# An identity, a split read and earlier input loads in the prologue of a Fourier filter with a token and channel mixer

## The chip, the cores and the metric

The kernel runs on one core of one Trainium2 chip. The metric is the device time of one execution in microseconds (us), taken on the chip. Executions of one and the same kernel scatter here by 3 to 10 us from the fastest to the slowest, that is 0.1 to 0.4%, so what follows is about differences near the edge of what can be measured. All runs told of here were in the fast state.

## The reference, cut to what matters

```python
def _attn_ref(x, filt_r, filt_i):            # x: 8 x 3008 x 256, float32
    X = np.fft.rfft(x, axis=1)
    Y = X * (filt_r + 1j * filt_i)[None]
    return np.fft.irfft(Y, n=x.shape[1], axis=1).astype(np.float32)

def _moe_ref(x, w_tok1, w_tok2, w_ch1, w_ch2):   # the four weights arrive as 64-bit floats
    xt = x.transpose(0, 2, 1)
    h = np.maximum(xt @ w_tok1, 0.0) @ w_tok2
    u = x + h.transpose(0, 2, 1)
    h2 = np.maximum(u @ w_ch1, 0.0) @ w_ch2
    return (u + h2).astype(np.float32)
```

First a filter along the 3008 tokens by way of a Fourier transform, then a mixer: two products along the tokens, and two along the channels.

## The kernel before

The transform is done as matmuls in two stages (3008 = 47 x 64). A batch's data go out to a buffer in device memory between the stages (`z_tmp`) and after the filter (`g_tmp`). The filter of batch 0 runs alone in the prologue. The filters of the later batches (in groups 1-2, 3-4, 5-6 and 7) are interleaved with the mixer of the batches before. In the prologue the 64-bit weights are also converted: each is split into two 32-bit floats, `top` and `rest`, whose sum is the weight. For most tiles TensorE makes this sum. The stationary matrix is `wai_t` for the first token weight, and an identity for the first six tiles of the second.

```python
def halves(st, n, pair):                      # one tile of 64-bit weights
    nc.scalar.activation(out=top, in_=hi_f, func=AF.Copy, scale=2.0 ** -112)          # ScalarE, L235
    yield
    nc.vector.tensor_scalar(...)                                                      # VectorE, L237
    ...                                                                               # three more, to L242

def on_chip(stat, top, rest, n, parts):
    banks.append(banks.pop(0))
    def f(tag=banks[0]):
        ps = bank(tag)
        m = ident[0] if stat is None else stat
        nc.tensor.matmul(ps[:, 0:n], m, top, start=True, stop=False)                  # L276
        nc.tensor.matmul(ps[:, 0:n], m, rest, start=False, stop=True)
        for src, dst in parts:
            nc.scalar.copy(out=dst, in_=src(ps))                                      # L279
    behind.append((ended[0] - 1, f))          # done two conversions later
...
def a_unit(b, c):                             # a "step" on one input block
    ps = bank(free_bank())
    nc.tensor.matmul(ps, wa, xs.pop((b, c))..., start=True, stop=True)                # L409
    nc.scalar.copy(out=t1..., in_=ps)                                                 # L411
    nc.scalar.dma_start(rows_of(z_d, b)[:, ts(c, XC), :], t1)
...
def t4_load(b, c, lo=0, hi=P):                # reads the filter's result, rows lo to hi, for the mixer
    if lo == 0:
        t4[b, c] = t4p.tile([P, TC4, D], FP32, tag="t4", name="t4")
    nc.sync.dma_start(t4[b, c][lo:hi], rows_of(g_d, b)[lo:hi, ts(c, TC4), :])
```

Rows 4k to 4k+3 of `t4` are ready when step k of the filter (`bi_unit(k)`, k = 0 to 31) has been written to `g_tmp`. The main part of the program:

```python
for i, _ in enumerate(dft(GROUPS[0])):        # the filter of batch 0; LAST_STEP = NXC + 2 + K2
    if i == 0:
        for t, src in ((wai_t, wait_d), (wai, wai_d)):
            nc.scalar.dma_start(t, src)
    ...                                        # conversions in between
        if LAST_STEP - 6 <= i < LAST_STEP:
            t4_load(0, i - LAST_STEP + 6, 0, EARLY_ROWS)        # rows 0 to 95, six reads of 384 KB
ident.append(t4p.tile([P, P], FP32, tag="t4", name="ident"))
nc.sync.dma_start(ident[0], ident_d)
second = dft(GROUPS[1])
next(second)                                   # first input blocks of batches 1 and 2
for c in range(A // TC4):
    t4_load(0, c, EARLY_ROWS)                  # rows 96 to 127
sum_up()
for i in range(rounds, A // 2 + TC * N2 // NG):
    convert()
    if i - rounds < XB:
        next(second)                           # a_unit
    if i == A // 2 + BY_PE - 1:
        sum_up()
        acc = token_sums(0)                    # L523, needs all of t4
...
for b, i, place in mix(next_ready):            # items of the mixer, three places in each
    ...
    if not done and (place == 1 or group == 0 and (spread or place == 2 and i % 2)):
        spread = next(todo, "end")             # a step of the next group's filter
        done = spread == "end"
```

DMAs of `nc.sync` are issued by SP, those of `nc.scalar` by ScalarE between its other instructions, and the filter's tables of batch 0 (`filt`) by GpSimd.

## Time and profile before

| | us |
|---|---|
| time, median of 3 runs | 2592.26 (2589.87 to 2595.21) |
| profiled span | 2587.8 |
| end of the filter of batch 0 on TensorE | 119.7 |
| first conversion on VectorE after it | 133.15 |
| token sums of batch 0 start | 139.54 |
| first mixer item starts | 171.28 |
| token sums of batch 1 start | 496.75 |

The rows below the span are times in the profiled run (from its start), and each kernel below is read at the same points. Where a later marker has moved by as much as an earlier one, nothing between them has been won or lost. The lines that carry the argument stand in the prediction.

### The profile page before, as it was taken

The page shows a single profiled execution, that of the slowest core. Times are in us where ns is not written, and L with a number is a line of the kernel's source. Part 1 is how long each engine was busy: PE and PEld are TensorE (multiplying, and loading weights), DVE is VectorE, ACT ScalarE, POOL GpSimd, SP SyncE. Part 2 cuts the span into 40 slices and gives each one's busy share as a digit, 9 for nine tenths or more (in the row PEclk, how much of TensorE's full clock was granted, in tenths as well). Part 3 has the DMA queues.
Part 4 walks back from the last instruction along what each step waited for, and adds up shares of the span by engine and source line. Part 5 has one row for each costly group of instructions (what it writes and reads, how often), then busy time and mean ns, then how long its engine had stood idle before and what let it go on. Part 6 is the DMA issues. An engine that isn't in the chain of part 4 may idle for free.

```text
span 2587.8 us, 31510 instructions
## 1 busy us (share of the span) xinstructions
PE 2506.3 (97%) x10952; PEld 2002.3 (77%) x10952; DVE 1795.6 (69%) x3441; ACT 691.4 (27%) x1347; POOL 524.7 (20%) x966
## 2 busy tenths in 40 slices
PE   5889999999999999999999999999999999999998
PEld 2456666788878777888787777788888888888887
DVE  3787888556675888746666788846678576647676
ACT  2433222123222222222321222212222122212222
POOL 3653111111211112112112111121121121211212
PEclk8999999999999999999999999999999999999999
DMA  8965333312332332202232223211232121100001
GB/s 235 263 190 166 107 106 107 94 48 87 93 90 63 88 86 73 80 17 89 90 96 78 75 84 87 80 31 57 90 85 75 50 64 52 25 9 8 17 12 21
DMA packets 156650, 211.43 MB, mean 82 GB/s; under 512 B 34552, under 2 KB 105314, under 8 KB 156492
## 3 DMA queue, kind: packets, MB, share of 16 engines
q1 hardware_dynamic: 84444, 118.86, 15.8%
q0 software_dynamic: 30656, 39.93, 6.4%
q10 hardware_dynamic: 41392, 50.62, 6.0%
q8 instruction: 87, 1.43, 0.2%
q14 instruction: 71, 0.58, 0.1%
HBM read 134.31 MB, written 74.97 MB: 81 GB/s over the span
## 4 chain that ended last, share of the span: by engine, by line
PE 80%; DVE 12%; DMA 3%; issue 2%; ACT 2%; ACTq 0%; SPq 0%; POOL 0%; DVEq 0%; POOLq 0%
PE ps_po L614 27%; PE ps_pg L580 16%; PE ps_pg L596 12%; PE ps_acc L540 4%; PE ps_acc L523 3%; PE ps_b L523 2%; DVE t L558 2%; PE ps_b L540 2%; PE ps_acc L477 2%; DVE hh L558 2%; PE ps_acc L545 2%; PE ps_b L452 2%; DVE u L558 2%; PE ps_b L409 2%; PE ps_b L477 1%
## 5 line engine op out<-in xcount | busy, mean ns | idle before, releaser
L558 DVE TENSOR_TENSOR hh<-ps_pg,s 128x512 f32<-128x512 f32 (+3 forms) x864 | 482.1, 585 | 622.6 <-ACT s L583 621.8
L659 POOL DMA_DIRECT2D out_dram<-r x757 | 409.8, 550 | 1943.5 <-ACT hh L601 921.0
L601 ACT ACTIVATE hh<-hh 128x512 f32<-128x512 f32 (+1 forms) x576 | 347.7, 621 | 1111.9 <-DVE hh L558 1111.9
L614 PE MATMUL ps_po<-t,wc 128*128 128x256 f32 (+1 forms) x2304 | 535.4, 375 | 5.4 <-DVE t L558 4.7
L614 PEld LDWEIGHTS ps_po<-t,wc 128*128 128x128 f32 x2304 | 434.4, 190 | 132.4 <-issue 54.0
L580 PE MATMUL ps_pg<-v,wc 128*128 128x256 f32 (+1 forms) x1728 | 416.0, 377 | 1.9 <-POOL wc L330 1.7
L614 PE MATMUL ps_po<-hh,wc 128*128 128x256 f32 (+1 forms) x1728 | 412.9, 375 | 0.2 <-ACT hh L601 0.2
L580 PEld LDWEIGHTS ps_pg<-v,wc 128*128 128x128 f32 x1728 | 328.5, 191 | 42.9 <-DVE v L558 3.0
L614 PEld LDWEIGHTS ps_po<-hh,wc 128*128 128x128 f32 x1728 | 328.2, 190 | 38.8 <-ACT s L583 0.8
L596 PE MATMUL ps_pg<-u,wc 128*128 128x256 f32 (+1 forms) x1152 | 293.2, 377 | 2.4 <-DVE hh L558 1.9
L558 DVE TENSOR_TENSOR t<-t,hh 128x256 f32<-128x256 f32 (+1 forms) x576 | 242.4, 421 | 19.8
L596 PEld LDWEIGHTS ps_pg<-u,wc 128*128 128x128 f32 x1152 | 215.9, 190 | 38.8 <-DVE hh L558 12.3
L558 DVE TENSOR_TENSOR s<-ps_pg,hh 128x512 f32<-128x512 f32 (+1 forms) x288 | 196.0, 681 | 30.7 <-PE ps_pg L580 0.9
L558 DVE TENSOR_TENSOR t<-hh 128x512 f32<-128x512 f32 (+1 forms) x288 | 191.9, 666 | 0.6 <-ACT hh L601 0.6
L580 PE MATMUL ps_pg<-u,wc 128*128 128x256 f32 (+1 forms) x576 | 170.4, 378 | 0.0
L596 PE MATMUL ps_pg<-v,wc 128*128 128x256 f32 (+1 forms) x576 | 168.8, 375 | 0.0
L583 ACT COPY s<-ps_pg 128x256 f32<-128x256 f32 (+1 forms) x288 | 105.8, 367 | 154.5 <-PE ps_pg L580 151.3
L596 PEld LDWEIGHTS ps_pg<-v,wc 128*128 128x128 f32 x576 | 108.7, 190 | 13.1
L580 PEld LDWEIGHTS ps_pg<-u,wc 128*128 128x128 f32 x576 | 102.8, 191 | 17.0 <-issue 8.4
L540 PE MATMUL ps_acc<-w,h 128*128 128x512 f32 (+1 forms) x228 | 106.2, 587 | 3.5 <-DVE w L263 2.8
L477 PE MATMUL ps_acc<-p,wb 128*96 128x256 f32 (+1 forms) x256 | 93.5, 466 | 7.5 <-DVE p L469 2.8
L523 PE MATMUL ps_b<-t,w 128*128 128x256 f32 x384 | 83.8, 380 | 1.3 <-ACT t L483 1.3
(92 smaller groups left out, 2251.8 us busy)
## 6 DMA issues: line engine op xcount, KB each, us to landing
z_tmp<-t ACTq DMA_DIRECT2D x96, 256.0 KB
t<-z_tmp SPq DMA_DIRECT2D x128, 192.0 KB
g_tmp<-t ACTq DMA_DIRECT2D x128, 192.0 KB
x<-in_x_dram SPq DMA_DIRECT2D x184, 128.0 KB
out_dram<-r POOLq DMA_DIRECT2D x698, 32.0 KB, 1.8
t<-g_tmp SPq DMA_DIRECT2D x42, 512.0 KB
wb<-wbi_t SPq DMA_DIRECT2D x80, 224.0 KB
filt<-in_filt_r_dram SPq DMA_DIRECT2D x128, 48.0 KB
```

The lines of the kernel that those rows point to most:

```text
L409: nc.tensor.matmul(ps, wa, xs.pop((b, c)).rearrange("p a d -> p (a d)"), start=True, stop=True)
L452: nc.tensor.matmul(ps, wbs[k // WC][0:KR, k % WC, 0:P], t2s[k // KC][:, k % KC], start=True, stop=True)
L477: nc.tensor.matmul(ps[0:KR], wbs[k // WC][:, k % WC, P:], p, start=(i == 0), stop=(i == len(parts) - 1))
L523: nc.tensor.matmul(acc[:, t, :], w1[:, a, ts(t, P)], t4[b, a // TC4][:, a % TC4, :], start=(a == 0 and t == 0), stop=(a == A - 1 and t == ...
L540: nc.tensor.matmul(ps[:, 0:w], h1[:, t, ts(dh, P)], w2[:, t, ds(m * 512, w)], start=(t == 0), stop=False)
L558: nc.vector.tensor_tensor(out=out, in0=in0, in1=in1, op=op)
L580: nc.tensor.matmul(ps[:, 0:hw], wc1[:, jp, n, :], mov, start=True, stop=True)
L583: nc.scalar.copy(out=s[:, 0], in_=g[0][:, 0, 0:hw])
L596: nc.tensor.matmul(ps[:, 0:hw], wc1[:, jp, n, :], mov, start=True, stop=True)
L601: nc.scalar.activation(out=hs, in_=hs, func=AF.Relu)
L614: nc.tensor.matmul(po[i][:, j, 0:hw], wc2[:, jp, n, :], mov, start=(jp == 0 and first == 1), stop=(jp == JP - 1 and last == 1))
L659: q.dma_start(rows[g, e, :, ds(h * A + 4 * m, n)], blocks[ts(g, CW), h, e, 0:n])
```

## The change

It removes the wait for the identity, has the mixer's first input read in three parts so that less is left to read when the filter ends, and issues the first input blocks of the second group before the last of these parts. A new rule for the steps in the mixer takes two input blocks in each of the items 0 to 3 instead of three.

```diff
-LAST_STEP = NXC + 2 + K2
-EARLY_ROWS = 96
+PARTS = (0, 64, 112)
...
+    ident = h1p.tile([P, P], FP32, tag="h1", name="ident")
...
-                where, tag = (h1p, "h1") if first and c % 3 == 2 else (t3p, "t3")
+                where, tag = (p2p, "p2") if first and c % 3 == 2 else (t3p, "t3")
...
+        second = dft(GROUPS[1])
         for i, _ in enumerate(dft(GROUPS[0])):
             if i == 0:
-                for t, src in ((wai_t, wait_d), (wai, wai_d)):
+                for t, src in ((wai_t, wait_d), (wai, wai_d), (ident, ident_d)):
                     nc.scalar.dma_start(t, src)
...
-                if LAST_STEP - 6 <= i < LAST_STEP:
-                    t4_load(0, i - LAST_STEP + 6, 0, EARLY_ROWS)
-        ident.append(t4p.tile([P, P], FP32, tag="t4", name="ident"))
-        nc.sync.dma_start(ident[0], ident_d)
-        second = dft(GROUPS[1])
-        next(second)
+                k = i - NXC - 2
+                if 19 <= k < 25:
+                    t4_load(0, k - 19, 0, PARTS[1])
+                elif k == 25:
+                    next(second)
+                elif k in (30, 31):
+                    for c in range(3):
+                        t4_load(0, 3 * (k - 30) + c, PARTS[1], PARTS[2])
         for c in range(A // TC4):
-            t4_load(0, c, EARLY_ROWS)
+            t4_load(0, c, PARTS[2], P)
...
-            if not done and (place == 1 or group == 0 and (spread or place == 2 and i % 2)):
+            if not done and (place == 1 or group == 0 and (spread and (place == 2 or i > 3) or place == 2 and i % 2)):
```

The cuts hold only what follows from these lines (`on_chip` gets `ident` as its stationary matrix). The change has four parts, called here the identity, the inputs ahead, the early reads, and the new rule.

> **What bounds the kernel now.** I read the page first. Its busy row says that TensorE is the bound over the span (97%), its clock row that only the first two of the 40 slices (65 us each) run below full clock, and its DMA row that the traffic is dense only there. Whatever the change can win lies in the prologue: the filter of the first batch, the conversion of the weights, and the first steps of the mixer.
>
> ```profile
> PE 2506.3 (97%) x10952; PEld 2002.3 (77%) x10952; DVE 1795.6 (69%) x3441; ACT 691.4 (27%) x1347; POOL 524.7 (20%) x966
> ...
> PE   5889999999999999999999999999999999999998
> ...
> PEclk8999999999999999999999999999999999999999
> DMA  8965333312332332202232223211232121100001
> ```
>
> Second, the timeline of TensorE (columns: start, duration, engine, line, operation, out<-in, shape, count; in brackets the idle time ahead of it and what ended it):
>
> ```profile
> 118.98 0.67 PE L477 MATMUL ps_acc<-p,wb 128*96 128x256 f32 x2 [0.15 <-DVE p L467]
> 126.52 1.62 PE L276 MATMUL ps_po<-both,ident 128*128 128x377 f32 x2 [6.86 <-DMA ident<-ident_t]
> ...
> 135.04 0.80 PE L276 MATMUL ps_po<-both,ident 128*128 128x377 f32 x2
> ...
> 139.54 20.88 PE L523 MATMUL ps_b<-t,w 128*128 128x256 f32 x96
> 161.12 1.12 PE L540 MATMUL ps_acc<-w,h 128*128 128x512 f32 x2 [0.69 <-ACT h L529]
> 165.02 1.13 PE L540 MATMUL ps_acc<-w,h 128*128 128x512 f32 x2 [2.78 <-DVE w L263]
> ```
>
> The filter ends at 119.6. The next matmul needs the identity and waits 6.86 us for it. The token sums (L523) then start at 139.54 with no wait of their own, but after them L540 waits for VectorE's converted weight. So the end of this stage is set by VectorE, and its timeline, with ScalarE's and the DMA queue's, says why it is late:
>
> ```profile
> 120.33 0.55 DVE L242 SCALAR_TENSOR_TENSOR both<-st,both 128x377 f32<-128x377 uint32 x1
> 133.15 0.36 DVE L237 TENSOR_SCALAR both<-both 128x377 uint32<-128x377 uint32 x1 [12.26 <-ACT both L235]
> ...
> 164.16 0.80 DVE L263 TENSOR_TENSOR w<-both 128x192 f32<-128x192 f32 x2
> ```
> ```profile
> 123.04 0.31 ACTq L488 DMA_DIRECT2D g_tmp<-t  x1
> 129.43 0.80 ACT L279 COPY w<-ps_po 128x384 f32<-128x384 f32 x1 [9.37 <-PE ps_po L277]
> 131.94 0.82 ACT L279 COPY w<-ps_po 128x384 f32<-128x384 f32 x1 [1.71 <-PE ps_po L277]
> 132.56 0.56 ACT L235 ACTIVATE both<-st 128x377 f32<-128x377 f32 x1
> ```
> ```profile
> 106.48 4.91 SPq L517 DMA_DIRECT2D t<-g_tmp  x6
> 112.06 0.34 SPq L776 DMA_DIRECT2D ident<-ident_t  x1
> 112.69 11.10 SPq L398 DMA_DIRECT2D x<-in_x_dram  x4
> 129.58 2.63 SPq L517 DMA_DIRECT2D t<-g_tmp  x6
> ```
>
> VectorE stands still for 12.26 us, because the next conversion's first step (ScalarE L235) is queued behind copies of the two sums (L279) that need the identity. From 133.15 VectorE works without a gap to 165, one weight tile each 2.62 us. The identity was issued at 112.06 behind six reads of 384 KB and used at 126.5: 14.4 us for 64 KB. In the merged chain it is the longest piece of the prologue.
>
> **What the Trainium skill says.** "DMA: Bandwidth & Descriptors", section "Queues, rings and completion order": within one queue an engine takes descriptors in order; and "Issuing engines are not separate DMA queues" there: all issuers share the same 16 engines. The trace agrees: 64 KB took 14.4 us where the DMA share between 106 and 120 us is 0.99. So where the identity is issued decides, not its size. The same page, "Rules for kernel authors", says not to split a transfer by partitions, as the parts use the same engines; here a split into three is made so that parts can start before their source is complete, and I expect from it an earlier last part, not more bandwidth. "TensorE: Matmul & The Clock Gate", "What's actually happening": an idle window of about 3.4 us halves the clock. The trace agrees: after the 6.86 us wait the two-matmul group takes 1.62 us, later 0.80.
>
> **The change part by part.**
>
> 1. The identity comes with the first tables, on ScalarE's queue. Added early: one issue (0.3 us of the ACT queue) and 64 KB at about 250 GB/s, 0.26 us, in a stretch where TensorE waits for transfers anyway: cost 0 to 0.5 us. Its buffer is the one that the filter's third output tile used; that tile goes to another single buffer, so nothing is lost. Removed: the wait. The filter ends at 119.6; two sums of 1.27 us each at full clock (135.04 to 136.31 for one) end at 122.2. Before, the second of these ended at 131.7 and VectorE restarted at 133.15, 1.45 us later. So VectorE restarts near 122.2 + 1.45 = 123.6, 9.5 us earlier. From there the chain of conversions is rigid (133.15 to 164.96), so L540 moves from 165.0 to about 155.5.
>
> 2. The token sums must not become the new bound. Three more conversions of 1.85 us after 123.6 allow them at about 129.5 + 0.3. Their last rows, 112 to 127, need the filter's last write. Before, ScalarE's issue of it stood at 123.04 although the tile was copied at 120.06; the order of the instructions with their waits shows that it waited for the landing of one of the big reads that shares its semaphore. After the change it shares with an earlier write, so I expect the issue at 120.4, the landing at about 124, the issue of six reads of 64 KB as long as that of the six before (2.63 us, as it goes by their number), and data at 127 to 129. Even if late: 129.8 + 20.9 + 1 = 151.7 against 155.5, so up to 4 us are hidden.
>
> 3. Reads of rows 0 to 63 (6 x 256 KB = 1.5 MB) move from 106-111 us to about 90-105, where the DMA share is 0.88 already: 0.12 x 18 us = 2.2 us free against 1.5 MB at 285 GB/s = 5.3 us. The filter's own loads may be pushed by some us, of which prefetch two pairs ahead hides most. Against it: the stall of VectorE for a filter table (1.88 us, near 114.9) that the burst before caused may go. I book a loss of 1 us, 0 to 3.
>
> 4. Second group's inputs: two blocks in at about 107 instead of 113-124, used at 122-124 now. No own gain.
>
> 5. In the mixer's first four items two input blocks instead of three are taken per item. Before, TensorE waited for inputs 2.96 us (182.4), 0.54 and 4.17 us (206.6), and two stretches of the items had clock 0.85 and 0.87. But VectorE is busy 11.53 of 12.03, 9.55 of 11.09 and 12.37 of 13.09 us in items 0 to 2, so these waits are mostly hidden: items 0 to 3 take 49.1 us and could take about 44.6. The four blocks that are put off cost 0.86 us each in items 4 to 7, where TensorE has no idle time: 3.4 us back. Net gain 1.1 us.
>
> 6. The first group's filter now ends one and two thirds items later. Before, the last inverse matmul ended at 479.3, the tiles of the next batch were read from 484 on, and its token sums started at 496.7. Now only the rest of one item and one whole item lie between the two: 1.7 + 1.5 + 1.1 + 1.1 + 1.5 = 6.9 us of matmuls by the timeline of such an item at 483 to 497. The first tile needs, as before, about 7.1 us from the end of the inverse matmul (copy 0.6, write and its landing 2.2, issue and read of 0.5 MB 4): 0 to 1 us lost, 0.5 booked.
>
> Sum: -9.5 + 0.3 + 1 - 1.1 + 0.5 = -8.8 us. 2592.26 - 8.8 = 2583.5; I say 2583.
>
> **The rivals.**
> A. The wait for the identity is replaced by one for the last rows of the mixer's input, because DMA is the true bound of 60 to 126 us (share 0.92 to 1.05). For it: density. Against it: the last part shrinks from 768 KB to 384 KB, and 4 us of slack. If true, the token sums start near 136 and the gain is 3 to 4 us: 2588.
> B. The earlier reads starve the filter: TensorE's small gaps at 60-115 grow by 3 to 5 us. For it: the share. Against it: total bytes up to 126 us are the same. Result 2586 to 2588.
> C. The input waits at 182 and 206 are worth their full size with the slow clock (about 11 us). For it: the chain of waits goes through these loads. Against it: VectorE's busy time above. Result 2575 to 2578.
> D. The order helps nothing as a late stage takes it all back. Nothing speaks for it: after 260 us TensorE is 93 to 97% busy and the order of work is fixed.
>
> **Range and chances.** Two runs of the kernel before differ by up to 5.3 us, so noise alone is 2 to 3 us. A and B pull up 4 us, C down 6. Range 2577 to 2588. A gain over 2% would be 52 us, more than all waits of the prologue after 119 us together; a loss over 2% would need a stall that I see nowhere. Faster 0.01, same 0.98, slower 0.01.
>
> **What would show it.** Right: no idle time ahead of L274 (the identity's matmul), VectorE's gap of 12.26 us shrunk to about 3, token sums starting at 129 to 132, the first L538 that waits for a converted weight near 155.5. A shows as a wait of L521 for the input tile; B as an end of the filter after 121; C as items 0 to 3 under 42 us. Point 6 shows as a wait of the second batch's token sums. I am wrong if the filter's end moves by more than 2 us or VectorE restarts later than 126.

## The result, and the profile after

| | before | after |
|---|---|---|
| median of 4 runs, us | 2593.66 (2589.87 to 2595.21) | 2592.15 (2589.95 to 2593.20) |
| ratio | | 0.9995, 95% interval 0.9978 to 1.0013 |

A ratio is the mean time of one kernel's fast runs over that of the other's fast runs of the same rounds, so it isn't quite the ratio of the medians. The times are the same, and 2592.15 lies outside the predicted range of 2577 to 2588.

The timeline of TensorE, of the kernel after (start, duration, engine, line, operation, out<-in, shape, count; in brackets the idle time ahead and what ended it). From `on_chip` on, lines are numbered two lower than before.

```profile
109.48 2.02 PE L475 MATMUL ps_acc<-p,wb 128*96 128x256 f32 x4 [2.69 <-ACT t L481]
...
125.53 1.10 PE L475 MATMUL ps_acc<-p,wb 128*96 128x256 f32 x4 [0.46 <-ACT t L481]
126.47 0.80 PE L274 MATMUL ps_po<-both,ident 128*128 128x377 f32 x2
...
139.31 22.64 PE L521 MATMUL ps_b<-t,w 128*128 128x256 f32 x96 [2.37 <-ACT both L235]
162.65 1.98 PE L538 MATMUL ps_acc<-w,h 128*128 128x512 f32 x4 [0.69 <-ACT h L527]
...
498.74 20.99 PE L521 MATMUL ps_b<-t,w 128*128 128x256 f32 x96 [0.81 <-DMA t<-g_tmp]
```

The same view of VectorE:

```profile
130.40 0.36 DVE L237 TENSOR_SCALAR both<-both 128x377 uint32<-128x377 uint32 x1 [2.88 <-ACT both L235]
...
161.38 0.80 DVE L263 TENSOR_TENSOR w<-both 128x192 f32<-128x192 f32 x2
```

The identity's matmul (L274) has no wait any more, and VectorE's gap has shrunk from 12.26 to 2.88 us. That is the gain that was predicted. But the filter now ends at 126.6 instead of 119.7, so VectorE restarts 2.75 us earlier and not 9.5. The token sums start only 0.2 us earlier and run in part at a slow clock (the clock that TensorE was granted was 0.50 of full from 139.8 to 143.2 us; the 96 matmuls take 22.64 us, before 20.88), and L538, which had waited 2.78 us for VectorE before, now waits for nothing but the token sums themselves. The first mixer item starts at 169.77 (before 171.28), and the second batch's token sums at 498.74 (before 496.75). A prologue 1.5 us shorter is followed by a stretch 3.5 us longer.

Why the filter ends later shows in the waits between 80 us and the filter's end (what waited and for what: us in total, times, longest). Before:

```profile
DVE p L466 <- DMA filt<-in_filt_i_dram: 1.9, 1, 1.9
...
PE ps_acc L477 <- ACT t L483: 1.0, 2, 0.6
```

After:

```profile
ACT filt L215 <- DMA filt<-in_filt_r_dram: 10.1, 6, 1.9
...
PE ps_acc L475 <- ACT t L481: 6.2, 6, 2.7
...
DVE p L464 <- DMA filt<-in_filt_i_dram: 3.7, 2, 2.1
```

ScalarE, which copies half of each filter table (L215), waits 10.1 us for tables to land, where before it waited for none in this stretch. Its instructions run in program order, so its copies of the filter's results (L481) come late, and TensorE waits 6.2 us (before 1.0) for them to free the bank. The transfers of these tables say the same (count, KB each, median us from issue to landing). Before, from 80 to 120 us:

```profile
filt<-in_filt_i_dram POOLq DMA_DIRECT2D x7, 48.0 KB, 4.0
...
filt<-in_filt_r_dram POOLq DMA_DIRECT2D x6, 32.0 KB, 3.3
```

After, from 80 to 127 us:

```profile
filt<-in_filt_i_dram POOLq DMA_DIRECT2D x7, 48.0 KB, 6.1
...
filt<-in_filt_r_dram POOLq DMA_DIRECT2D x7, 32.0 KB, 5.2
```

And what the early reads meet there: the stretch from 88 to 106 us in the view of windows (window, its us, then busy us and instructions of TensorE, its weight loads, VectorE, ScalarE and GpSimd, the granted clock, DMA share, GB/s), before and after:

```profile
88.00:106.00 18.00, 16.91 (x63) 10.21 (x61) 16.75 (x38) 8.83 (x19) 16.06 (x29) 1.00 0.88 247
```
```profile
88.00:106.00 18.00, 15.94 (x58) 9.71 (x59) 14.11 (x32) 7.66 (x17) 13.09 (x25) 1.00 1.02 269
```

The DMA share (the packets' times as a share of 16 engines' span, so that it can pass 1) goes from 0.88 to 1.02, and every engine gets less done in the same 18 us: 63 against 58 matmuls, 38 against 32 instructions of VectorE.

A part of the delay comes from a slower TensorE. From the end of its wait of 2.69 us (matmuls again at 109.48) its granted clock was half of full for 6.83 us, in the same view of windows:

```profile
109.05:115.88 6.83, 6.40 (x13) 4.01 (x14) 4.39 (x10) 1.72 (x4) 4.87 (x9) 0.50 1.06 259
```

It was busy for 6.40 us of these; as an estimate from this line, the same matmuls would have taken up to 3.2 us less at full clock. All four kernels with the early reads (they are told of below) have 6.8 us at half clock between 100 us and the filter's end, and the seven with no read as early have none there.

The way to the token sums after the filter is next. The DMA queue of SP and the DMA queue of ScalarE, after:

```profile
122.58 14.07 SPq L515 DMA_DIRECT2D t<-g_tmp  x12
```
```profile
127.07 0.31 ACTq L486 DMA_DIRECT2D g_tmp<-t  x1
```

The filter's last write is issued right when its tile is copied, as predicted. But the reads behind it are issued up to 136.65, and the token sums have to wait for their data: 139.3 instead of the predicted 129.8. The profile puts this wait to ScalarE's L235, which ended last, at 139.27. By the trace's semaphores L521 waited for the first of the six late reads, whose last piece landed at 139.18, and by the program it needs nothing of L235. What SP's queue waited for between 80 and 145 us (columns as for the waits above):

```profile
SPq L515 <- DMA g_tmp<-t: 18.6, 5, 7.3
```

The longest single wait for a write to `g_tmp`, 7.3 us, is the one for the last write, which landed at 133.98, 6.9 us after its issue. The prediction had booked 3.6 us for this.

### The profile page after: what moved, and what is told of

It reads as the page before. It is cut to its first block, busy times and chain, and to the rows that moved or that the text cites. A ratio compares the mean times of both kernels' runs of the same rounds, so it can differ in the third digit from the quotient of the medians.

```text
span 2590.2 us, 31521 instructions
## 1 busy us (share of the span) xinstructions
PE 2510.2 (97%) x10952; PEld 2002.7 (77%) x10952; DVE 1795.7 (69%) x3441; ACT 691.2 (27%) x1347; POOL 527.7 (20%) x966
## 4 chain that ended last, share of the span: by engine, by line
PE 76%; DVE 12%; ACT 2%; issue 2%; DMA 1%; ACTq 0%; DVEq 0%; POOL 0%; SPq 0%; POOLq 0%
PE ps_po L612 27%; PE ps_pg L578 16%; PE ps_pg L594 11%; PE ps_b L538 4%; PE ps_b L521 3%; DVE t L556 3%; DVE hh L556 2%; PE ps_acc L521 2%; PE ps_acc L538 2%; PE ps_b L543 2%; PE ps_acc L407 2%; DVE u L556 2%; PE ps_acc L475 1%; PE ps_b L475 1%; DVE s L556 1%
## 5 line engine op out<-in xcount | busy, mean ns | idle before, releaser
L521 PE MATMUL ps_b<-t,w 128*128 128x256 f32 x480 | 106.3, 384 | 3.2 <-ACT both L235 2.4
L538 PE MATMUL ps_b<-w,h 128*128 128x512 f32 (+1 forms) x232 | 107.7, 587 | 0.0
```

Source lines behind the costliest of these rows:

```text
L521: nc.tensor.matmul(acc[:, t, :], w1[:, a, ts(t, P)], t4[b, a // TC4][:, a % TC4, :], start=(a == 0 and t == 0), stop=(a == A - 1 and t == ...
L538: nc.tensor.matmul(ps[:, 0:w], h1[:, t, ts(dh, P)], w2[:, t, ds(m * 512, w)], start=(t == 0), stop=False)
```

## The experiments

Theory: the early reads put 1.5 MB on the DMA engines while the filter's tables are being fetched, and the longer filter eats what the early identity wins. Rival one: it is the inputs issued ahead, also in the filter's time, that lengthen it. Rival two: the prologue is better, and the new rule in the mixer gives the gain back. Each run below has a ratio to the kernel before, taken on the same chip in the same call with five rounds. Medians of before were 2593.18 (first four runs), 2592.0 (next four) and 2592.6 (last two). All results were correct.

### The identity alone

The kernel before, with only this part:

```diff
+    ident = h1p.tile([P, P], FP32, tag="h1", name="ident")
-                where, tag = (h1p, "h1") if first and c % 3 == 2 else (t3p, "t3")
+                where, tag = (p2p, "p2") if first and c % 3 == 2 else (t3p, "t3")
-                for t, src in ((wai_t, wait_d), (wai, wai_d)):
+                for t, src in ((wai_t, wait_d), (wai, wai_d), (ident, ident_d)):
-        ident.append(t4p.tile([P, P], FP32, tag="t4", name="ident"))
-        nc.sync.dma_start(ident[0], ident_d)
```

> The kernel before with one part of the change: the identity comes with the first tables (and the third output tile moves to the other single buffer). Theory (the early reads of the mixer's input starve the filter of its tables; the identity is a gain by itself): the filter ends at 119.6 us as before (within 1), VectorE restarts its conversions at 123.5 to 126.5 instead of 133.15, the mixer's first step starts at 162 to 166 instead of 171.3, and the time falls by 5 to 9 us, to 2584 to 2588. Rival 1 (the early identity itself, by shifting which transfers share a semaphore, delays the filter): the filter ends at 124 or later and the time falls by less than 3 us. Rival 2 (the last rows of the mixer's input are the next bound): the token sums still start at 138 to 140, after a wait for the input tile, and the mixer's first step at 169 or later.

Measured: 2590.85 us, ratio 0.9992 (0.9980 to 1.0005). The filter ends at 118.6 and VectorE restarts at 122.38, as the prediction's first step has it. The first item was expected at 162 to 166 and the time at 2584 to 2588: both were missed, the item starts at 170.62. For then comes another wait. TensorE, VectorE and ScalarE of this run:

```profile
127.12 2.04 PE L408 MATMUL ps_b<-x,wa 128*128 128x512 f32 x2 [5.94 <-DMA x<-in_x_dram]
```
```profile
130.87 0.36 DVE L238 TENSOR_SCALAR both<-both 128x377 uint32<-128x377 uint32 x1 [6.56 <-ACT both L236]
```
```profile
129.20 0.59 ACT L410 COPY t<-ps_b 128x512 f32<-128x512 f32 x1 [6.85 <-PE ps_b L408]
```

The wait for the identity had hidden one for the second group's first input block. TensorE waits 5.94 us for `x`. ScalarE's copy of the result (L410) stands in the queue ahead of the next conversion's first step (L236), so VectorE stands still for 6.56 us. Two waits lie in series here, and taking away one alone gives about 2 us, which this interval doesn't tell from nothing.

### The whole change with the old rule

```diff
-            if not done and (place == 1 or group == 0 and (spread and (place == 2 or i > 3) or place == 2 and i % 2)):
+            if not done and (place == 1 or group == 0 and (spread or place == 2 and i % 2)):
```

> The changed kernel with the old rule for the steps of the second group's filter (three input blocks per item from the first item). Theory (the new rule costs 3 to 4 us between the mixer's first step and the second batch's token sums: 329.0 us of it after, 325.5 before): the stretch is back at 324 to 327 us and the time is 2 to 5 us under the changed kernel's, 2587 to 2590; the prologue to the mixer's first step stays at 170, within 1.5. Rival (the new rule is a gain as I predicted, and the stretch grew for another cause, such as the shifted start of the weights): the stretch stays at 328 us or more, and the time is at or above 2592.

Measured: 2588.68 us, ratio 0.9988 (0.9975 to 1.0000). Its filter ends at 128.4. So the long filter has nothing to do with the rule, and the rule isn't what takes most of the gain: without it 3 us are left of the predicted 9, and even these the interval hardly tells from nothing. The stretch from the first item to the second batch's token sums is 326.8 us, as expected; the first item, at 171.98, is 0.5 us later than the range given for it.

### The new rule alone

The kernel before, with the line above changed the other way.

> The kernel before with the new rule for the second group's steps alone. Theory (the rule costs by itself): the mixer's first step at 171.3 as before, the stretch from there to the second batch's token sums 328 to 330 us instead of 325.5, time up 2 to 5 us, 2595 to 2598. Rival (what I predicted, less waiting for inputs): the stretch falls to 324 to 325 and the time falls by about 1 us.

Measured: 2596.94 us, ratio 1.0020 (1.0007 to 1.0032): slower by some 5 us, where the prediction had booked 0.6 us in its favour. The stretch from the first item to the second batch's token sums takes 329.5 us, against 325.5 before. Over all twelve kernels, the three with the new rule have 328.0 to 329.5 us there, and the nine with the old one 323.6 to 326.9. The windows of this stretch, of the kernel before and of the whole change, say where (items 0 to 3; items 4 to 8; items 9 to 28; item 29 up to the token sums; columns as above). Before:

```profile
171.28:220.40 49.12, 38.98 (x135) 26.52 (x134) 43.48 (x76) 18.76 (x33) 36.58 (x63) 0.93 0.70 211
220.40:262.18 41.78, 41.26 (x171) 31.58 (x170) 29.39 (x58) 14.45 (x27) 5.16 (x10) 1.00 0.47 148
262.18:468.69 206.51, 196.90 (x777) 139.81 (x776) 174.82 (x303) 52.59 (x100) 34.72 (x64) 1.00 0.36 102
468.69:496.75 28.06, 25.71 (x121) 21.88 (x121) 21.78 (x44) 6.95 (x15) 0.00 (x0) 1.00 0.48 164
```

After:

```profile
169.77:216.81 47.04, 33.94 (x127) 23.00 (x126) 43.86 (x77) 15.97 (x29) 38.85 (x62) 0.98 0.57 179
216.81:262.76 45.95, 44.57 (x178) 33.09 (x177) 27.71 (x56) 15.94 (x30) 4.63 (x10) 0.98 0.48 154
262.76:466.24 203.48, 194.32 (x771) 138.53 (x770) 170.46 (x297) 52.32 (x100) 34.78 (x64) 1.00 0.38 106
466.24:498.74 32.50, 29.83 (x128) 22.94 (x127) 27.88 (x53) 8.86 (x18) 0.00 (x0) 1.00 0.17 52
```

Items 0 to 3 win 2.1 us, not 4.5. VectorE is busy 43.9 of 47.0 us there, so it sets the pace, and TensorE, idle for 10.1 us before, is idle for 13.1 after. The input blocks that were put off had mostly filled idle time of TensorE: leaving them out saved 2.1 us. In items 4 to 8 they cost 4.2 us (41.8 to 46.0). In items 9 to 28, 3.0 us less are spent, but 4.4 us more from item 29 to the token sums, as the filter's last steps slide there. In sum +3.5 us. The run with the new rule alone shows the same four differences: -2.4, +4.9, -3.0 and +4.5 us.

### The whole change with the inputs issued where they were

```diff
-                elif k == 25:
-                    next(second)
...
+        next(second)
         for c in range(A // TC4):
             t4_load(0, c, PARTS[2], P)
```

> The changed kernel with the second group's first inputs issued after the filter's loop, as before. It tells which of the two early transfers lengthens the filter (it ends at 119.6 before, at 126.6 after). Theory (the 1.5 MB of early reads of rows 0 to 63 do it): the end stays at 124 to 127. Rival (the four input loads, which hold the in-order issuing queue from 105 to 112 us ahead of the filter's own next loads): the end falls to 119.5 to 122. Time within 3 us of the changed kernel's by the theory, 3 to 6 under it by the rival.

Measured: 2601.38 us, ratio 1.0035 (1.0021 to 1.0048). The filter still ends at 126.4, so rival one falls: the inputs aren't what makes it 7 us longer. A small share isn't excluded: without early reads the filter ends at 119.8 to 123.6 with the inputs ahead, and at 118.6 to 122.4 without. The expectation for the time was a miss. The kernel is 9 us slower than the whole change, because the second of the two waits is back, of TensorE:

```profile
137.01 2.05 PE L407 MATMUL ps_b<-x,wa 128*128 128x512 f32 x2 [8.09 <-DMA x<-in_x_dram]
```

### Identity and inputs ahead, without the early reads

The edit of the first experiment, and this (the new rule is left out too):

```diff
+        second = dft(GROUPS[1])
         for i, _ in enumerate(dft(GROUPS[0])):
...
+                if i == LAST_STEP - 7:           # k = 25
+                    next(second)
                 if LAST_STEP - 6 <= i < LAST_STEP:
                     t4_load(0, i - LAST_STEP + 6, 0, EARLY_ROWS)
-        second = dft(GROUPS[1])
-        next(second)
```

> The kernel before with the identity among the first tables and the second group's first inputs issued one step ahead of the reads of the mixer's input; these reads in two parts and at their old places, old rule of steps. Theory (identity and inputs are two waits in series on the path to VectorE's conversions, and only the early reads lengthen the filter): the filter ends at 118 to 122.5, VectorE has no gap above 3.5 us after it (12.3 before, 2.5 and 6.6 with the identity alone), the mixer's first step starts at 162 to 167, and the time is 2583 to 2587. Rival (the last rows of the mixer's input come too late for the token sums and take the gain): the token sums start after 136 with a wait for the input tile, the mixer's first step is at 168 or later and the time 2588 or more.

Measured: 2582.26 us over six runs (2579.27 to 2586.27), ratio 0.9962 (0.9949 to 0.9974). This version is 9.9 us faster than before, and beats both kernels. Its filter ends at 119.8, VectorE restarts at 123.59 and has no gap again before its conversions end. All this is as the theory expected, and the time is 0.7 us under the range given. VectorE and TensorE of this run:

```profile
123.59 0.36 DVE L238 TENSOR_SCALAR both<-both 128x377 uint32<-128x377 uint32 x1 [2.53 <-ACT both L236]
```
```profile
133.14 22.64 PE L522 MATMUL ps_b<-t,w 128*128 128x256 f32 x96 [3.00 <-DMA t<-g_tmp]
156.47 1.98 PE L539 MATMUL ps_acc<-w,h 128*128 128x512 f32 x4 [0.69 <-ACT h L528]
```

The token sums wait 3.00 us for the last rows (the last write of the filter took 8.5 us to land) and run in part at the slow clock, and L539 is held by them: they end at 155.8, where VectorE's conversions end at 155.35. So the slack of 4 us that the prediction had found is used up, and some of the win with it: VectorE restarts 9.6 us earlier than before, and the first item, at 163.59, starts 7.7 us earlier.

### The early reads alone

The kernel before, with the reads of the change (rows 0 to 63 at k = 19 to 24, rows 64 to 111 at k = 30 and 31, the rest after the filter).

> The kernel before with the reads of the mixer's input in three parts alone (rows 0 to 63 while the filter runs), identity and inputs late, old rule of steps. Theory (these reads lengthen the filter by their 1.5 MB): the filter ends at 125 to 128.5, as in the three runs that have them, and the mixer's first step comes at 174 or later, the time is 2594 to 2600. Rival (it takes the combination with another part): the filter ends under 123.

Measured: 2599.04 us, ratio 1.0024 (1.0012 to 1.0036), +6.2 us, as expected. The filter ends at 127.5. TensorE of this run:

```profile
112.05 2.02 PE L477 MATMUL ps_acc<-p,wb 128*96 128x256 f32 x4 [3.46 <-ACT t L483]
...
126.42 1.10 PE L477 MATMUL ps_acc<-p,wb 128*96 128x256 f32 x4 [0.46 <-ACT t L483]
```

The order of waits is that of the whole change, with single waits that are longer: ScalarE waits 3.58 us for a table, TensorE 3.46 us for ScalarE's copy, and then TensorE's clock is at half for 6.83 us. (From 88 to 106 us this run has 63 matmuls, as many as before, so the slower work that the whole change shows there isn't common to all.) Four kernels have these reads (the whole change, the second and fourth experiments, and this), and their filters end at 126.4 to 128.4. Seven have no read as early, and end at 118.6 to 123.6. That the early reads lengthen the filter is shown; a single look can't give the size better than some 3 us, as before and the kernel with the new rule alone have the same prologue and end it at 119.7 and 122.4. The tables tell the two groups apart as well: from 80 us to the filter's end, their median times to landing are 4.7 to 6.2 us in the four and 3.2 to 4.4 us in the seven, and ScalarE waits for tables for 5.2 to 10.1 us in all in the four and for 0 to 3.3 us in the seven.

### Three parts, none of them early

Identity and inputs ahead, with `EARLY_ROWS = 64`, and behind the filter:

```diff
         for c in range(A // TC4):
-            t4_load(0, c, EARLY_ROWS)
+            t4_load(0, c, EARLY_ROWS, 112)
+        for c in range(A // TC4):
+            t4_load(0, c, 112)
```

> As the run with identity and early inputs, but the reads of the mixer's input in three parts, none earlier than before: rows 0 to 63 at the old places, 64 to 111 and 112 to 127 after the filter. It tells whether a smaller last part is worth anything. Theory (the last part is not on the path, as VectorE's conversions are): the mixer's first step within 1.5 us of that run's, time within 1.5 us. Rival (the token sums are held by the last part's landing): it starts 2 us earlier or more.

Measured: 2588.29 us over six runs, ratio 0.9986 (0.9973 to 0.9999). It is 6 us slower than the version in two parts, which was not expected: a miss. The filter ends at 120.0, so nothing is lost there. ScalarE of this run:

```profile
122.05 1.47 ACT L278 COPY w<-ps_po 128x384 f32<-128x384 f32 x2 [1.69 <-DMA t<-g_tmp]
...
130.65 0.34 ACTq L411 DMA_DIRECT2D z_tmp<-t  x1
131.09 0.54 ACT L236 ACTIVATE both<-st 128x377 f32<-128x377 f32 x1 [6.77 <-DMA t<-g_tmp]
```

ScalarE stands still for 6.77 us until one of the reads has landed, and VectorE waits 5.86 us for it. Just before it lies ScalarE's issue of a store to `z_tmp`, at 130.65, and it is this issue that waited: it shares a semaphore with the first of the twelve reads, whose last piece landed at 130.57. ScalarE needs none of the rows itself. So a read that is put behind the filter isn't free either.

### Identity and inputs ahead, the inputs six steps earlier

`LAST_STEP - 13` in place of `LAST_STEP - 7` (k = 19).

> As the run with identity and early inputs, but the inputs six filter steps earlier. 0.5 MB in a stretch in which the DMA engines are 0.85 to 0.9 busy. Theory (any bulk read ahead of the filter's own tables delays it in proportion: 1.5 MB cost 7 us): the filter ends 0 to 2.5 us later than in that run and the time is the same within 2 us. Rival (the harm came from where the reads stood, not from their bytes): the filter's end is the same within 0.5 us.

Measured: 2584.45 us, ratio 0.9971 (0.9960 to 0.9983). The profiled filter ends 3.8 us later than with k = 25, more than the 0 to 2.5 us expected, but within the scatter of single looks. No gain from going earlier is seen.

### Identity and inputs ahead, with a quarter of the early reads

Rows 48 to 63 are read at k = 19 to 24 (six reads of 64 KB), rows 0 to 47 and 64 to 95 where rows 0 to 95 were.

```diff
+                k = i - NXC - 2
+                if 19 <= k < 25:
+                    t4_load(0, k - 19, 48, 64)
...
-                    t4_load(0, i - LAST_STEP + 6, 0, EARLY_ROWS)
+                    t4_load(0, i - LAST_STEP + 6, 0, 48)
+                    t4_load(0, i - LAST_STEP + 6, 64, EARLY_ROWS)
```

> As the run with identity and early inputs (filter's end 119.8 us), plus six reads of rows 48 to 63 alone at the places where the changed kernel reads rows 0 to 63: as many issues in the in-order queue, waiting for the same writes of the filter, but 64 KB each instead of 256 KB. It tells by which way the early reads lengthen the filter. Theory (by their bytes: they take DMA time from the filter's tables): a quarter of the bytes, so the filter ends at 119.5 to 122.5. Rival (by their waits: the queue stands still for the filter's write and the filter's own next loads stand behind): the filter ends at 125 to 128, as in the four runs with 256 KB each.

This asks whether it is the bytes or the waits that early issues bring with them (SP issues in order, and each early read waits for a write of the filter). Measured: 2584.78 us, ratio 0.9967 (0.9954 to 0.9981), which isn't told apart from the version without early reads. The filter ends at 123.1, at the upper edge of the group without them and 3 us under the group with all the bytes. Its tables land as in the kernels without early reads (medians 3.9 to 4.4 us). The same six issues with a quarter of the bytes don't do what the full ones did, so the bytes carry most of it. A share of the waits isn't excluded: ScalarE still waits 6.0 us in all for tables, TensorE waits 2.22 us for a part of `wb`, the filter's stationary matrices, which SP's queue brings, and then has half its clock for 3.4 us. The edit also makes twelve reads out of six at the old place.

### The inputs ahead alone

The kernel before with the diff shown at the fifth experiment, and the identity late as it was.

> The kernel before with the second group's first inputs issued ahead, identity late: the fourth corner beside the kernel before, identity alone and both. Theory (two waits in series: removing either leaves the other): VectorE's gap after the filter stays at 10 to 13 us, ended by the identity, the mixer's first step at 169 to 173 and the time within 3 us of the kernel before, while both together gave 9 us. Rival (the inputs were the true bound and the identity adds nothing): the mixer's first step at 166 or earlier.

Measured: 2593.66 us, ratio 1.0002 (0.9989 to 1.0014), the same as before, as expected. TensorE of this run:

```profile
132.44 1.62 PE L276 MATMUL ps_po<-both,ident 128*128 128x377 f32 x2 [8.92 <-DMA ident<-ident_t]
```

Now it is the identity that TensorE waits for, 8.92 us, and VectorE's gap after the filter is 13.68 us. The profiled run was the slowest of its kernel (2596.51), and its first item, at 178.2, is later than expected. The four kernels together: neither 0, the identity alone -2, the inputs alone +0.5, both -9.9 us. Neither part has a gain of its own; each uncovers the other's wait.

## Why the prediction was wrong

The effects in order, each by the difference of two ratios times 2592, so with intervals of some 4 to 6 us either way: identity -2.1; inputs ahead, on top of it, -7.8; early reads, on top of both, +6.7; new rule +1.8. In sum -1.3 us, where -8.8 was predicted. Of the difference, step 3 makes some 5.7 us (+6.7 in place of +1) and steps 5 and 6 some 2.4 us (+1.8 in place of -0.6). That the time would be the same within 2% had been given a chance of 0.98 and came true, but that says nothing of the steps.

1. *The identity's wait.* The mechanism and its size were right: 9.5 us predicted; with the inputs ahead VectorE restarts 9.6 us earlier and the time is 9.9 us shorter (some 3 us either way). But it was put down to the identity alone. That 9.9 meets 9.5 so well is in part luck: the two profiled runs differ by 7.6 us, as their first items do.
2. *The token sums must not become the new bound.* The order of the last write and the reads was right (the issue at 127.07, as the copy ended). The times were too good: the last write took 6.9 us to land and not 3.6, data were expected some 7 to 9 us after the filter's end, and the token sums started 12.7 us after it, with a slow clock at first. The 4 us of slack took up most of this in the version without the early reads, whose first item starts 7.7 us earlier and not 9.5.
3. *The earlier reads.* This step failed: "I book a loss of 1 us, 0 to 3". They cost 6.7 us (6.2 alone). The sum of bytes over free share was worked out for the whole stretch, 2.2 us free against 5.3 us needed, and then the difference of 3 us was taken to be hidden by tables fetched two pairs ahead. It wasn't hidden: the tables landed 2 us later each, and ScalarE waited six times for them, 10.1 us in all; TensorE waited for ScalarE, and its clock fell to half for 6.8 us. Rival B had this, at 2586 to 2588, and it was put aside with "total bytes up to 126 us are the same". That was true and beside the point, as the bytes came at a time when small transfers that the filter waits for had to share the DMA engines with them.
4. *Second group's inputs: "No own gain."* Right to the letter (+0.5 alone) and wrong in what it led to: without them step 1 gains 2 us.
5. *Fewer input blocks in the first items.* Predicted -4.5 and +3.4, measured -2.1 and +4.2. The prediction saw that VectorE was the bound there ("busy 11.53 of 12.03"), and yet took 4.5 us as to be had by taking work from TensorE.
6. *The end of the first group's filter.* Predicted 0.5 us of loss. The 0.81 us wait for the tile is there, but the stretch from item 29 on grew by 4.4 us, offset by 3.0 us in the items before. Steps 5 and 6 together: -0.6 predicted, +3.5 in the trace.

Two small slips in the prediction change nothing: its clock row shows one slice below full clock and not two, and three conversions of 1.85 us after 123.6 end at 129.2 and not 129.5.

Of the rivals, A came true in part: the token sums waited for their input in both versions. C fell with step 5. Both signs that the prediction named for its own failure showed: the filter ends 7 us later (the limit was 2), and VectorE restarts at 130.4 (the limit was 126).

What stays open: how much of the early reads' cost comes through the waits of SP's queue rather than through bytes, how much of it is the slow clock, and the exact size of the new rule in the whole change, where the traces say 3.5 us and the ratios 1.8.

## What to carry to other kernels

When a wait is removed, look for the next wait on the same engine that ended at about the same time, and remove both in one change, or the first measures as nothing. A bulk read that is moved forward must be checked against the small transfers that set the pace at its new place: free share of the DMA engines on the average doesn't protect them. An engine that looks idle in a stage where another engine sets the pace does filler work there cheaply (here the four blocks cost 2.1 us there and 4.2 us later), so don't move that work to a stage where it is the bound.

## What the Trainium skill lacked or had wrong

- "DMA: Bandwidth & Descriptors", section "Queues, rings and completion order", says that each DMA engine goes round robin between queues by packets. That section gives no times for small transfers beside bulk ones. Here tables of 48 and 32 KB on GpSimd's queue went from landing medians of 4.0 and 3.3 us to 6.1 and 5.2 when 1.5 MB on SP's queue were moved into the same stretch, and the stage that they feed ended 7 us later.
- The same page, section "Anatomy of one DMA — SWDGE (gpsimd) path", says that a wait on a semaphore happens on the issuing sequencer. It lacks the consequence for an engine that also computes: the issue of a store held ScalarE for 6.77 us in the run with three late parts, and the conversions behind it.
- "TensorE: Matmul & The Clock Gate", section "What's actually happening", gives an idle window of about 3.4 us as what lowers the clock. Here less was enough: after waits of 2.37 and 3.00 us the granted clock was 0.50 for 3.41 us, and the 96 matmuls took 22.64 us in place of 20.88. In the 3.41 us before the clock fell TensorE had been busy for 1.04 and 0.54 us. After the wait of 2.78 us in the kernel before, the clock stayed at 1.00.
